# A parallel attention and GELU block: two dense groups side by side in the stretch without direct scores, an earlier fetch and another order at the end

## The chip, the cores and the metric

The kernel runs on one core of one Trainium2 chip. The metric is the device time of one execution in microseconds; of several runs the median is shown. Engines are called as in the profile: PE (matrix products), PEld (its weight loads), DVE, ACT and POOL (elementwise work), SP (which here only issues DMAs).

## What is computed

The block adds an attention and a dense part to its input. With S = 2048 rows, D = 512 columns, 32 heads of 16 columns and 1792 hidden columns:

```python
xn = layernorm(x)
q, k, v = split_heads(xn @ wqkv)                 # 32 heads, 16 columns each
p = softmax(q @ k.T * 16 ** -0.5)                # per head, 2048 x 2048
out = x + merge_heads(p @ v) @ wo + gelu(xn @ w1 + b1) @ w2 + b2
```

## The kernel before

Values that go through fp16 products are held as a high and a low half (`PAIRS`: high·high, high·low, low·high), so each product of a chunk of 128 rows is three products.

Heads go in 8 groups of four (`NG`), queries in 4 blocks of 512 (`NQB`). A pair of both is called `t`, 0 to 31; each has 16 key tiles, so there are `NU` = 512 units. A call of `unit` writes the work of one position `pos` in two halves, a = 0 and a = 1. In each half it writes, for the position's unit u, two direct scores `s_half` (tile pS, whose maxima DVE takes), for the unit 20 positions back (`LEAD`) two transposed scores `e_half` (tile pT, exponentiated by ACT into `pe`), and for a unit one or two positions further back `v_half`: the product of `pe` with the values, summed over all 16 key tiles in one bank, tile pV. Each of these uses 64 rows of the PE array and four column strips, hence four matmuls of 64x32; matmuls on rows 0 to 63 and on rows 64 to 127 are separate. In a half, pV uses the one row half.

The other row half gets `dense` work: a `Group` is one output tile in one PSUM bank, a sum over products. Its products on rows 0 to 63 and those on rows 64 to 127 are issued in alternate halves, into the same bank. `FAST`, `MEAN`, `SLOW` and `LATE` say how many half-width products a half gets, (12, 12) in the stretch after the last direct scores, so six full-width products, with four in front of pV and two behind it (`BEHIND`). One group is open at a time (`cur`). When a sum passes from one row half to the other, the first product there waits on a semaphore until the last one of the half before is done: `leave` marks the last product of a user, `enter` and `product` set the wait, for the users "V" (the pV sum) and "D" (the dense group).

PSUM has eight banks: three for tiles pS, three or four for pT, one each for a dense group and pV, passed around by `banks` and `hold`. Late dense groups take pS banks, so their tile is named pS.

Instructions stand on each engine in the order in which the code writes them. `later` and `tick` move an action some positions on, `when` does it once a head block's result is in DRAM.

The last generator of groups, `tail`, is the output projection. For a block qb of 512 rows and q in 0..3, `o_proj` multiplies the heads' result `oc` by `wo_s`. DVE adds it to `ac`, which holds the rest of the output (`finish`), and SP stores it. For blocks 2 and 3 the last 64 columns (the last heads) come too late for this, so they have a second, short group of three products, `o_end`, which reads `ol` (block 2, loaded from DRAM by `rows`) or `last` (block 3, kept in SBUF). The last head block is turned by `last_one`: four transposes, DVE's reciprocal and multiply, four transposes, ACT's and DVE's split into halves `ot`. After the last position `land` issues what is left of the open group, each row half by itself with a drain of PE ahead, and `burst` and `drain` issue whole groups on all 128 rows.

Of the kernel before, what the change touches and what calls it, by code (L numbers as in the profile page):

```python
# [18 lines left out]
S = 2048  # L19
D = 512  # L20
# [6 lines left out]
QB = 512  # L27
# [3 lines left out]
LEAD = 20  # L31
FAST, MEAN, SLOW, LATE = (8, 8), (7, 7), (6, 6), (12, 12)
MEASURE = (3, 0, 1, 2)
HALF = 1300
BEHIND = 4
POOL_NS = 2500
TAIL = 5
LFILL = (8, 16, 12, 12)
# [10 lines left out]
def layer_kernel(ctx: ExitStack, tc: tile.TileContext, x, wqkv, wo, w1, b1, w2, b2, out):  # L49
# [114 lines left out]

    turns = {u: tc.alloc_semaphore("turns" + u) for u in "VD"}
    counted, left, newest, goal = {"V": 0, "D": 0}, {}, {}, {}

# [45 lines left out]
    def later(n, fn, local=False):  # L213
        queue.append((slot[0] + n, fn, local))
# [105 lines left out]
    def v_end(u):  # L320
# [12 lines left out]
        if t == NG * NQB - 1:  # L333
            later(1, lambda: last_one(osb))
            return
# [40 lines left out]
    def last_one(osb):  # L376

        on = work.tile([P, 4, 4, DH], F32, name="on")
        rden = work.tile([P, 4, 4], F32, name="rden")
        pq = banks("S")  # L380
        for q in range(4):
            nc.tensor.transpose(pq[:, q * P:(q + 1) * P], osb[:, q * P:(q + 1) * P], ident)
        pqv = pq.rearrange("p (q h e) -> p q h e", q=4, h=4)
        nc.vector.reciprocal(rden, pqv[:, :, :, DH])
        nc.vector.tensor_tensor(on, pqv[:, :, :, 0:DH], rden.unsqueeze(3).to_broadcast([P, 4, 4, DH]), op=ALU.mult)
        pt = banks("S")
        for q in range(4):
            nc.tensor.transpose(pt[:64, q * P:(q + 1) * P], on[:, q].rearrange("p h d -> p (h d)"), ident)
        ot = work.tile([P, 2, QB], F16, name="ot", bufs=2)
        nc.scalar.activation(ot[:64, 0], pt[:64, :], AF.Copy)  # L390
        nc.vector.tensor_tensor(ot[:64, 1], pt[:64, :], ot[:64, 0], op=ALU.subtract)
        last.append(ot)

# [13 lines left out]
    def dbank():  # L407
        turn[0] += 1
        if pos[0] < LEAD:
            return banks("T"), None  # L410
        if pos[0] > NU:
            return banks("S"), None
        return hold("D", "T")

    class Group:
# [19 lines left out]
        def product(self, side, parts=2):  # L435
# [16 lines left out]
            assert not start or n == 2  # L452
            tiled("D", self.bank[:, cols], lhs[r], rhs[r][:, cols], start, self.last and self.over())
            return n
# [97 lines left out]

    pos, spent, cur = [0], [False], [None]
    feed, xbs, wcs = [], {}, {}
# [11 lines left out]

    def group(gen):

        if cur[0] is None and not spent[0]:
            cur[0] = next(gen, 0)  # L570
            if cur[0] == 0:
                cur[0], spent[0] = None, True
        return cur[0]

    def ended():

        if cur[0] is not None and cur[0].over():
            done, cur[0] = cur[0], None
            done.end()

    def burst(gen, n):

        while n > 0 and (f := group(gen)) is not None:
# [28 lines left out]
    def unit(gen):  # L612
# [7 lines left out]
        for a in range(2):  # L620
# [5 lines left out]
            if e >= 0:  # L626
# [8 lines left out]

                for user, goes_on in (("V", live and not (r == 1 and w % 16 == 15)),
                                      ("D", cur[0] is not None and not cur[0].over())):
                    leave(user, goes_on)
                for k in backlog:
# [484 lines left out]
    with ExitStack() as st3:  # L1124
# [8 lines left out]
        def fetch(qb):  # L1133
# [9 lines left out]
            for k in range(4 * qb, 4 * qb + 4):  # L1143
                if k not in acs:
                    acs[k] = p3.tile([P, D], F32, name=f"ac{k}")
                    later(2 + k % 4, lambda k=k: read_acc(acs[k], k))

        def tail():
            for qb in (2, 0, 3, 1):
                fetch(qb)  # L1150
            for qb in (2, 0, 3, 1):
                while qb != 2 and qb not in known:
                    yield None
                for q in range(4):
                    yield o_proj(qb, q, qb >= 2)

            def rows():
                nc.sync.dma_start(ol, ot_d[D - 64:, :, 2 * QB:3 * QB])
                known.add(2)

            when((NG - 1) * NQB + 2, rows)
            while 2 not in known:
# [12 lines left out]
        land()  # L1175
        while queue or steps:
            tick()
            burst(fil, TAIL)
        drain(fil)

# [26 lines left out]
```

## Time and profile before

| what | us |
|---|---|
| median of 3 runs (lowest, highest) | 1502.55 (1499.8, 1506.8) |
| profiled execution, its own time | 1504.39 |
| its span on the core | 1502.6 |
| PE busy | 1471.0 |
| DVE busy | 1374.5 |
| ACT busy | 1231.7 |
| POOL busy | 716.6 |

The span runs from the first to the last instruction of the profiled execution. The time of an execution holds a little more than the span. The mean granted clock of PE is 0.994 of full speed. Direct scores end about 1412 us into the span, the transposed scores at about 1469. A row of a timeline gives the start, the duration of the merged instructions, the engine, the line, what is written and read, and how many instructions; in brackets stands the idle time of the engine before and what ended it.

### The profile page before, as it was taken

To read this page: it belongs to the slowest core of one execution; us is meant where nothing else is said; L and a number is where in the kernel's file an instruction comes from. 1 tells how busy PE (TensorE), PEld (TensorE's weight loads), DVE (VectorE), ACT (ScalarE), POOL (GpSimd) and SP (SyncE) were. 2 spreads that over 40 slices of the span, in tenths; PEclk is the share of its full clock that TensorE was granted. 3 is DMA by queue.
4 is the path that set the end of the run, shared out by engine and by line. 5 is a ranking of instruction groups with operands and counts; after the bars stand their busy time and mean duration, and the time that the engine had idled before them with its cause. 6 is when DMAs were issued, how large, how long until landed. Compare 5 with 4: busy or idle time off the path is not lost.

```text
span 1502.6 us, 87920 instructions
## 1 busy us (share of the span) xinstructions
PE 1471.0 (98%) x39971; PEld 931.1 (62%) x39971; DVE 1374.5 (91%) x2372; ACT 1231.7 (82%) x2326; POOL 716.6 (48%) x750
## 2 busy tenths in 40 slices
PE   8998999999999999999999999999999999999997
PEld 4434566666666666666666666666666666666653
DVE  7898989999999999999999999999999999999612
ACT  5315878899999889989998998998899999988771
POOL 4113597547665545537553554665264465511000
PEclk9999999999999999999999999999999999999998
DMA  6454476633211311121112211121112111022412
GB/s 207 129 172 139 160 217 221 196 116 94 71 37 44 89 43 37 36 68 54 36 51 59 63 37 37 35 83 57 37 43 63 53 32 35 23 68 81 152 35 89
DMA packets 113677, 123.82 MB, mean 82 GB/s; under 512 B 24988, under 2 KB 85276, under 8 KB 113304
## 3 DMA queue, kind: packets, MB, share of 16 engines
q1 hardware_dynamic: 113304, 118.21, 25.5%
q8 instruction: 312, 5.11, 1.4%
q14 instruction: 61, 0.50, 0.1%
HBM read 80.61 MB, written 37.34 MB: 78 GB/s over the span
## 4 chain that ended last, share of the span: by engine, by line
PE 81%; DVE 13%; DMA 2%; issue 2%; SPq 1%; ACT 1%; POOL 0%; ACTq 0%; POOLq 0%
PE pV L170 22%; PE pD L170 20%; PE pS L170 19%; PE pT L170 17%; DVE mt L259 11%; PE pT L444 1%; PE pS L444 1%; DVE amx L679 1%; PE pT L543 1%; PE pD L444 1%; DMA m_d<-mhl 1%; PE pV L543 0%; SPq L1080 0%; DMA xs<-in_A_x_dram 0%; DVE mneg L270 0%
## 5 line engine op out<-in xcount | busy, mean ns | idle before, releaser
L259 DVE TENSOR_REDUCE mt<-pS 128x1 f32<-128x512 f32 x2048 | 1274.3, 683 | 37.4 <-PE pS L170 22.4
L304 ACT ACTIVATE pe<-pT 128x512 f32<-128x512 f32 x2048 | 1107.0, 600 | 153.3 <-PE pT L170 79.2
L170 PE MATMUL pV<-pe,vv 64*32 64x512 f32 x8192 | 1093.1, 599 | 1.1 <-issue 1.0
L170 PE MATMUL pT<-qst,kst 64*32 64x512 f16 x8192 | 668.5, 377 | 3.5 <-ACT pe L304 1.8
L170 PE MATMUL pS<-kst,qst 62*32 62x512 f16 x8192 | 632.7, 379 | 8.7 <-DVE mt L259 6.1
L170 PE MATMUL pD<-xb,wc 64*32 64x512 f16 x5376 | 372.1, 375 | 0.0
L170 PE MATMUL pD<-w_s,g 64*32 64x512 f16 (+1 forms) x6144 | 362.0, 348 | 0.0
L170 PEld LDWEIGHTS <-qst 62*32 62x32 f16 x8192 | 248.1, 92 | 140.6 <-issue 49.5
L170 PEld LDWEIGHTS <-kst 64*32 64x32 f16 x8192 | 251.8, 93 | 101.4 <-issue 13.9
L170 PEld LDWEIGHTS <-g 64*32 64x32 f16 x6144 | 196.1, 92 | 85.3 <-issue 0.7
L170 PEld LDWEIGHTS <-wc 64*32 64x32 f16 x5376 | 177.4, 91 | 98.4
L170 PEld LDWEIGHTS pV<-pe,vv 64*32 64x32 f32 x8192 | 172.5, 105 | 6.0 <-issue 2.2
L1022 POOL TENSOR_SCALAR hh<-hh,fac,b_s 128x512 f32<-128x512 f32 x56 | 43.0, 768 | 265.3 <-ACT hh L1020 265.3
L170 PE MATMUL pD<-xt,wqk_h 64*32 64x512 f16 x1920 | 129.8, 377 | 3.1 <-issue 3.0
L360 POOL TENSOR_TENSOR osb<-osb,rb 128x512 f32<-128x512 f32 x31 | 39.8, 1283 | 140.1 <-DMA rb<-den_d 101.9
L1049 POOL TENSOR_TENSOR xa<-xa,yt 128x512 f32<-128x512 f32 x32 | 41.1, 1283 | 108.4 <-ACT yt L1047 108.4
L170 PEld LDWEIGHTS <-wqk_h 64*32 64x32 f16 x1920 | 61.8, 92 | 27.7 <-issue 3.6
L1086 DVE SCALAR_TENSOR_TENSOR ac<-pS,gs,ac 128x512 f32<-128x512 f32 x20 | 15.0, 751 | 66.1 <-PE pS L170 57.2
L993 POOL TENSOR_TENSOR t<-t,hh 128x512 f32<-128x512 f32 x56 | 71.8, 1283 | 4.7
L1000 POOL TENSOR_TENSOR t<-t,hh 128x512 f32<-128x512 f32 x56 | 71.7, 1281 | 4.7
L995 POOL TENSOR_TENSOR g<-t,g 128x512 f16<-128x512 f32 x56 | 65.2, 1164 | 4.7
L170 PE MATMUL pS<-wo_s,oc 64*32 64x512 f16 x1008 | 62.6, 377 | 0.4
(140 smaller groups left out, 926.3 us busy)
## 6 DMA issues: line engine op xcount, KB each, us to landing
wch<-in_B_w_dram SPq DMA_DIRECT2D x28, 512.0 KB
wc<-w_d SPq DMA_DIRECT2D x56, 256.0 KB
qk_d<-stg SPq DMA_DIRECT2D x32, 256.0 KB
rb<-den_d SPq DMA_DIRECT2D x124, 64.0 KB
w_d<-wsp SPq DMA_DIRECT2D x28, 256.0 KB
kst<-qk_d SPq DMA_DIRECT2D x128, 48.0 KB
qst<-qk_d SPq DMA_DIRECT2D x128, 48.0 KB
xs<-in_A_x_dram SPq DMA_DIRECT2D x16, 256.0 KB
```

The lines of the kernel that those rows point to most:

```text
L170: p = nc.tensor.matmul(*args, **kw)
L259: nc.vector.reduce_max(mt_of[t][:, n, qt, kb:kb + 1], s, axis=AX.X)
L304: nc.scalar.activation(pe, st, AF.Exp, scale=factor(exp_scale, sexp[0:1, g // 2:g // 2 + 1]))
L360: pooled((1280, lambda: nc.gpsimd.tensor_tensor(osb, osb, rb, op=ALU.mult)), (620, lambda: nc.gpsimd.tensor_scalar(ot[:, 0], osb, 1.0, 0.0 ...
L444: nc.tensor.matmul(self.bank, lhs, rhs, start=start, stop=self.last and self.over())
L543: nc.tensor.matmul(pj, xt[:, i, c, t * P:(t + 1) * P], wh[j][:, c, :], start=(n == 0), stop=(n == 11))
L679: nc.vector.tensor_reduce(dst, v, axis=AX.XY if len(v.shape) == 3 else AX.X, op=ALU.max, apply_absolute_value=True)
L993: (1280, lambda: nc.gpsimd.tensor_tensor(t1, t1, hh, op=ALU.mult)),
L995: (1160, lambda: nc.gpsimd.tensor_tensor(g[:, 1, f, :], t1, g[:, 0, f, :], op=ALU.subtract)),
L1000: (1280, lambda: nc.gpsimd.tensor_tensor(t1, t1, hh, op=ALU.mult)),
L1022: later(1, lambda: pooled((690, lambda: nc.gpsimd.tensor_scalar(hh, hh, scale, bias, op0=ALU.mult, op1=ALU.add)), (0, lambda: gelu(hh, g, ...
L1049: add = lambda: nc.gpsimd.tensor_tensor(xa, xa, yt, op=ALU.add)
```

## The change

There are three edits.

1. `cur` holds two groups. After the last direct scores (`pos[0] > NU + 1`) `dense` writes three full-width products (`LATE` = 6 halves) of the first group, then pV, then three of the second, all on the same row half. A pair of groups has a user each, "D" and "E", with a semaphore and waits of its own. A lane opens a new group only where four more positions are left. `land` keeps no drain.
2. The DMA of `ol` is no longer asked for after all groups of `o_proj`, but at the start of `tail`, as soon as its rows are in DRAM.
3. `last_one` is a generator with three parts. After the last position, twelve products (`TAIL`), its first part, twelve products, its second part, then the rest of `tail` and, in a generator of its own, the four groups that read `last`.

```diff
-FAST, MEAN, SLOW, LATE = (8, 8), (7, 7), (6, 6), (12, 12)
+FAST, MEAN, SLOW, LATE = (8, 8), (7, 7), (6, 6), 6
-TAIL = 5
+TAIL = 12
...
-    turns = {u: tc.alloc_semaphore("turns" + u) for u in "VD"}
+    turns = {u: tc.alloc_semaphore("turns" + u) for u in "VDE"}
...
-            later(1, lambda: last_one(osb))
+            last.append(last_one(osb))
...
         nc.vector.tensor_tensor(on, pqv[:, :, :, 0:DH], rden.unsqueeze(3).to_broadcast([P, 4, 4, DH]), op=ALU.mult)
+        yield
         pt = banks("S")
...
-        last.append(ot)
+        last[0] = ot
+        yield
...
         if pos[0] > NU:
+            if free_banks["D"]:
+                free_banks["S"].append(free_banks["D"].pop())
             return banks("S"), None
...
-            tiled("D", self.bank[:, cols], lhs[r], rhs[r][:, cols], start, self.last and self.over())
+            tiled("DE"[cur.index(self)], self.bank[:, cols], lhs[r], rhs[r][:, cols], start, self.last and self.over())
...
+    def some_of(f, side, n, until=0):
+
+        while f is not None and n > until and f.usable(side):
+            n -= f.product(side, n)
+        return n
+
     def dense(gen, side, between=lambda: None):
 
+        if pos[0] > NU + 1:
+            fs = [group(gen, k) if cur[k] is not None or pos[0] + 4 <= NU + LEAD + 2 else None for k in range(2)]
+            some_of(fs[0], side, LATE)
+            between()
+            some_of(fs[1], side, LATE)
+            return
         f = group(gen)
-        n = 0 if f is None else (f.pace if pos[0] <= NU + 1 else LATE)[pos[0] % 2]
-        behind = 0 if f is not None and f.ends(n) else BEHIND
-        while n > behind and f.usable(side):
-            n -= f.product(side, n)
+        n = 0 if f is None else f.pace[pos[0] % 2]
+        n = some_of(f, side, n, 0 if f is not None and f.ends(n) else BEHIND)
         between()
-        while n > 0 and f.usable(side):
-            n -= f.product(side, n)
+        some_of(f, side, n)
+
+    def pass_on():
+
+        for lane, user in enumerate("DE"):
+            leave(user, cur[lane] is not None and not cur[lane].over())
 
     def land():
 
-        if cur[0] is not None:
+        for k in range(2):
             enter()
-        for side in range(2):
-            while cur[0] is not None and cur[0].left(side):
-                nc.tensor.drain()
-                while cur[0].left(side):
-                    cur[0].product(side)
+            for lane, f in enumerate(cur):
+                while f is not None and f.left((k + lane) % 2):
+                    f.product((k + lane) % 2)
+            pass_on()
         ended()
...
+        def rows():
+            nc.sync.dma_start(ol, ot_d[D - 64:, :, 2 * QB:3 * QB])
+            known.add("rows")
+
         def tail():
             for qb in (2, 0, 3, 1):
                 fetch(qb)
+            when((NG - 1) * NQB + 2, rows)
...
-            while not last:
-                yield None
+
+        def end():
             for q in range(4):
                 yield o_end(3, q, last[0])
...
         land()
+        for _ in range(2):
+            burst(fil, TAIL)
+            next(last[0])
+        drain(fil)
+        fil, spent[0] = end(), False
+        drain(fil)
         while queue or steps:
             tick()
-            burst(fil, TAIL)
-        drain(fil)
```

How the instructions move is shown at three places. On PE, in one half of a late position, the rows before are these (each weight load and matmul of a dense product stands four times; pS here is the dense group's bank, oc3 the heads' result of block 3). The first fence runs from one pV to the next half's first product.

```order
L170 MATMUL pS_48552<-wo_s_116,oc3_46698 32x512 [waits turnsD]
...
L170 MATMUL pV_48271<-pe_48506,vv_113 32x512 [waits turnsV]
...
L170 LDWEIGHTS oc3_46698
...
L170 MATMUL pT_48665<-qst1_1_3_112,kst1_1_1_94 32x512 [waits Activation_49]
...
L170 MATMUL pT_48672<-qst1_1_3_112,kst1_1_1_94 32x512 [waits Activation_49]
```

Sixteen matmuls of the group stand ahead of pV there and eight behind it. In the changed kernel a half reads so:

```order
L170 MATMUL pS_48490<-wo_s_116,oc3_46698 32x512 [waits turnsD]
...
L170 MATMUL pV_48296<-pe_48531,vv_113 32x512 [waits turnsV]
...
L170 MATMUL pS_48593<-wo_s_116,oc3_46698 32x512 [waits turnsE]
...
L170 MATMUL pT_48690<-qst1_1_3_112,kst1_1_1_94 32x512 [waits Activation_49]
...
L170 MATMUL pT_48697<-qst1_1_3_112,kst1_1_1_94 32x512 [waits Activation_49]
```

Now twelve matmuls of one bank stand ahead of pV and twelve of another behind it, with a wait of their own. On PE after the last position, before (ident marks transposes, wo_l the weights of the last 64 columns):

```order
L382 MATMUL pS_49607<-ident_74,osb_49527 128x128 x4
L388 MATMUL pS_49614<-ident_74,on_49605 64x128 x4
L444 LDWEIGHTS oc1_46703
L444 MATMUL pS_49622<-wo_s_116,oc1_46703 128x512
...
L444 MATMUL pS_49638<-wo_l_46663,ol_46665 128x512
...
L444 MATMUL pS_49662<-wo_l_46663,ot_49619 128x512
```

and now:

```order
L448 MATMUL pS_49505<-wo_s_116,oc1_46703 128x512
...
L382 MATMUL pS_49522<-ident_74,osb_49503 128x128 x4
L448 LDWEIGHTS oc1_46703
L448 MATMUL pS_49529<-wo_s_116,oc1_46703 128x512
...
L389 MATMUL pS_49544<-ident_74,on_49520 64x128 x4
L448 LDWEIGHTS ol_46665
L448 MATMUL pS_49552<-wo_l_46663,ol_46665 128x512
...
L448 MATMUL pS_49576<-wo_l_46663,ot_49549 128x512
```

Twelve products on all rows moved ahead of the first transposes and twelve between both. Ahead of the first transposes there stood 80 matmuls on single row halves. On SP before, from the write of the last heads' rows to the output stores:

```order
L367 DMA ot_d_72<-ot_48945 32x1x512 x4
L1089 DMA out_0_dram<-ac4_46704 128x512
L1089 DMA out_0_dram<-ac5_46705 128x512
L1089 DMA out_0_dram<-ac6_46706 128x512
L1089 DMA out_0_dram<-ac7_46707 128x512
L1158 DMA ol_46665<-ot_d_72 64x2x512
```

and now:

```order
L367 DMA ot_d_72<-ot_48994 32x1x512 x4
L1166 DMA ol_46665<-ot_d_72 64x2x512
L1106 DMA out_0_dram<-ac4_46704 128x512
L1106 DMA out_0_dram<-ac5_46705 128x512
L1106 DMA out_0_dram<-ac6_46706 128x512
L1106 DMA out_0_dram<-ac7_46707 128x512
```

The fetch of `ol` moved from behind four output stores to ahead of them.

More of the change, by code (lines that the diff above doesn't have):

```diff
@@ L161, in given @@
         backlog[engine] += ns
-    turns = {u: tc.alloc_semaphore("turns" + u) for u in "VD"}
-    counted, left, newest, goal = {"V": 0, "D": 0}, {}, {}, {}
+    turns = {u: tc.alloc_semaphore("turns" + u) for u in "VDE"}
+    counted, left, newest, goal = dict.fromkeys("VDE", 0), {}, {}, {}
     def product(user, *args, **kw):
@@ L551, in run @@
             pass
-    pos, spent, cur = [0], [False], [None]
+    pos, spent, cur = [0], [False], [None, None]
     feed, xbs, wcs = [], {}, {}
@@ L565, in fetch_w1, with group @@
             nc.sync.dma_start(wcs[n], w1_d[n % NF // 2, :, n % 2])
[L567 to L573, printed above, removed]
+    def group(gen, lane=0):
+        if cur[lane] is None and not spent[0]:
+            cur[lane] = next(gen, 0)
+            if cur[lane] == 0:
+                cur[lane], spent[0] = None, True
+        return cur[lane]
     def ended():
-        if cur[0] is not None and cur[0].over():
-            done, cur[0] = cur[0], None
-            done.end()
+        for lane, f in enumerate(cur):
+            if f is not None and f.over():
+                cur[lane] = None
+                f.end()
     def burst(gen, n):
@@ L634, in unit @@
                     v_half(w, r)
-                for user, goes_on in (("V", live and not (r == 1 and w % 16 == 15)),
-                                      ("D", cur[0] is not None and not cur[0].over())):
-                    leave(user, goes_on)
+                leave("V", live and not (r == 1 and w % 16 == 15))
+                pass_on()
                 for k in backlog:
@@ L1155, in tail @@
                     yield o_proj(qb, q, qb >= 2)
[L1157 to L1162, printed above, removed]
+            while "rows" not in known:
                 yield None
```

1 line of the change is left out of this document (added).

## The prediction

> **What bounds the kernel now.** I read the page first, then the windows over the end of the span, then the matmuls of one late unit in order of time, then everything after the last score.
>
> ```profile
> span 1502.6 us, 87920 instructions
> PE 1471.0 (98%) x39971; PEld 931.1 (62%) x39971; DVE 1374.5 (91%) x2372; ACT 1231.7 (82%) x2326; POOL 716.6 (48%) x750
> PE 81%; DVE 13%; DMA 2%; issue 2%; SPq 1%; ACT 1%; POOL 0%; ACTq 0%; POOLq 0%
> ```
>
> PE is the bound, but "98% busy" counts a PE on which one of the two row halves (rows 0 to 63 and 64 to 127 of the array, used by separate matmuls) works while the other stands. So I price units, not busy time. A unit issues 16 pV matmuls, so the count of pV in a window gives the length of a unit. The rows below are the windows, for tile pV alone, of the stage with direct scores and of the late stretch without them:
>
> ```profile
> 1300.00:1400.00 100.00, 81.30 (x616) 12.97 (x608) 0.00 (x0) 1.84 (x3) 1.00 0.28 85
> 1421.07:1468.98 47.91, 34.02 (x260) 5.02 (x256) 0.00 (x0) 0.60 (x1) 1.00 0.17 56
> ```
>
> 616/16 = 38.5 units in 100 us, 2.60 us each; 260/16 = 16.25 units in 47.91 us, 2.95 us each. The late unit has no direct scores and is slower. Why, the PE timeline of one late half shows (start, us, what):
>
> ```profile
> 1440.02 0.40 PE L170 MATMUL pT<-qst,kst 64*32 64x512 f16 x4
> 1440.27 0.40 PE L170 MATMUL pS<-wo_s,oc 64*32 64x512 f16 x4
> 1440.34 0.63 PE L170 MATMUL pV<-pe,vv 64*32 64x512 f32 x4
> 1440.49 0.61 PE L170 MATMUL pS<-wo_s,oc 64*32 64x512 f16 x8
> 1440.78 0.61 PE L170 MATMUL pV<-pe,vv 64*32 64x512 f32 x4
> 1440.92 0.61 PE L170 MATMUL pS<-wo_s,oc 64*32 64x512 f16 x8
> 1441.21 0.40 PE L170 MATMUL pT<-qst,kst 64*32 64x512 f16 x4
> 1441.35 0.40 PE L170 MATMUL pS<-wo_s,oc 64*32 64x512 f16 x4
> 1441.57 0.40 PE L170 MATMUL pT<-qst,kst 64*32 64x512 f16 x4
> 1441.82 0.40 PE L170 MATMUL pS<-wo_s,oc 64*32 64x512 f16 x4
> ```
>
> Dense products (pS<-wo_s,oc, four matmuls each) start 0.215 us apart (two between 1440.49 and 1440.92). The sixth starts at 1441.35 and takes about 0.38; the first of the next half starts at 1441.82, 0.09 after its end, although the transposed scores of its row half were issued at 1441.21 and held that row half for 0.215 only. That is the wait on "turnsD": the next half of the group adds to the same bank from the other row half and waits until the last product is done. A half is thus 5 x 0.215 + 0.38 + 0.09 = 1.55 us, two make 3.1; units whose second half has only three products bring the mean to 2.95.
>
> The end, all engines (rows left out are other weights and matmuls):
>
> ```profile
> 1474.74 0.61 PE L170 MATMUL pV<-pe,vv 64*32 64x512 f32 x4
> 1474.86 5.32 PE L170 MATMUL pS<-wo_s,oc 64*32 64x512 f16 x80
> ...
> 1480.11 0.66 PE L382 MATMUL pS<-ident,osb 128*128 128x128 f32 x4
> 1480.23 0.75 DVE L1086 SCALAR_TENSOR_TENSOR ac<-pS,gs,ac 128x512 f32<-128x512 f32 x1 [5.30 <-PE pS L170]
> 1480.89 0.25 DVE L384 RECIPROCAL rden<-pS 128x16 f32<-128x16 f32 x1
> 1481.75 0.60 PE L388 MATMUL pS<-ident,on 128*64 128x128 f32 x4 [0.98 <-DVE on L385]
> 1482.18 2.75 PE L444 MATMUL pS<-wo_s,oc 128*128 128x512 f16 x12
> 1482.38 0.59 ACT L390 ACTIVATE ot<-pS 64x512 f16<-64x512 f32 x1 [6.32 <-PE pS L388]
> 1483.06 0.68 DVE L391 TENSOR_TENSOR ot<-pS,ot 64x512 f16<-64x512 f32 x1 [1.46 <-DMA out_dram<-ac]
> ...
> 1486.25 0.56 SPq L1158 DMA_DIRECT2D ol<-ot_d x1
> 1489.06 4.48 PE L444 MATMUL pS<-wo_l,ol 64*128 64x512 f16 x12 [4.13 <-DMA ol<-ot_d]
> ...
> 1493.34 5.32 PE L444 MATMUL pS<-wo_l,ot 64*128 64x512 f16 x12
> ...
> 1498.70 0.75 DVE L1086 SCALAR_TENSOR_TENSOR ac<-pS,gs,ac 128x512 f32<-128x512 f32 x1 [0.53 <-PE pS L444]
> ```
>
> The last pV ends its stream at 1475.17 (the second pass at 1474.74 plus 0.43). From there to the end of the span are 27.4 us: twenty products on one row half at a time, a chain of transposes with PE waiting, then PE stands 4.13 us for the rows "ol", and the 24 products after that take 0.43 each where the twelve before (2.75 us) took 0.215. The windows over that place tell why (PE, PEld, DVE, ACT, POOL busy, then clock, DMA share, GB/s):
>
> ```profile
> 1486.00:1488.00 2.00, 0.00 (x0) 0.00 (x0) 0.00 (x0) 0.00 (x0) 0.00 (x0) 1.00 0.47 156
> 1490.00:1492.00 2.00, 2.00 (x6) 0.67 (x5) 1.42 (x2) 0.00 (x0) 0.00 (x0) 0.50 0.24 88
> 1494.00:1496.00 2.00, 2.00 (x6) 0.69 (x5) 1.08 (x2) 0.00 (x0) 0.00 (x0) 0.50 0.66 249
> ```
>
> After the idle stretch the granted clock is 0.50.
>
> **The change, part by part.** *Two groups in the late stretch.* The number of products per half stays six, three of one group before pV and three of another behind it, so nothing is removed or added but one semaphore wait per half. When a group's turn comes again, its last product lies behind three products of the other group, or behind pT, three products and pV, over 0.65 us back against the 0.47 (0.38 + 0.09) that it needs: both waits are over when they are reached. What then bounds the unit is a row half: six products, two pT and one pV (0.88 from first pass to the next matmul, 1440.34 to 1441.21), 8 x 0.215 + 0.88 = 2.60 us. The stage with direct scores puts the same on a row half (four products, two pS, two pT, one pV) and reaches exactly 2.60, with as many matmuls in a unit (80); so I take 2.60.
>
> ```profile
> 1440.31 1.08 ACT L304 ACTIVATE pe<-pT 128x512 f32<-128x512 f32 x2 [0.26 <-PE pT L170]
> ```
>
> ACT, at two exponentials in 1.08, needs 2.2 us per unit and stays hidden. 16.25 units x 0.35 = -5.7 us. Against it: two open groups and the last heads' pV leave one bank to turn over, and three groups (the third of block 0, the first two of block 3) begin in a bank whose sum DVE still has to read (0.38 + 0.75 + 0.1 = 1.2 us after the last product starts, about 1.0 away): 3 x 0.2 = +0.6. After the last transposed score at 1468.98 four pV halves are left, now 6.2 us paced by products; then each waits only for the pV before it (0.44 + 0.61 + 0.09 = 1.15): 0.3 + 3 x 1.15 + 0.88 = 4.6, -1.6. Together -6.7. Not known is how far PE passes the waits of the middle group; the ends are 0 for the units (+0.6 - 1.6 = -1.0) and, with no bank wait, -7.3. I take the upper one because the 2.60 row is the nearest.
>
> *Groups that end with the units, and twelve products between the steps of the last chain.* Nothing is left to land on single row halves, and the two drains there meet no work. After the last pV PE runs 12 full products (2.6), the four transposes (0.5), 12 products (2.6), four transposes (0.5), then 12 on "ol" and 12 on "ot". ACT's copy of the pV bank (0.6) and DVE's reciprocal and multiply lie behind the products; without that cover they would cost about 2 us. Step by step from the last pV: transposes of "on" start at 5.7; transposes to the end of DVE's "ot" took 1481.75 to 1483.74, so "ot" is done at 7.7; DVE queues the eight last sums behind it. DVE instructions back to back start 0.66 apart (1480.23, 1480.89), PE needs 0.65 per group of three, so the eighth sum ends at 7.7 + 7 x 0.66 + 0.75 = 13.1. From the end of the last sum to the end of the span were 3.15 us (1499.45 to 1502.6). Eight stores of 0.26 MB at 0.66 us ask for 397 GB/s; the row at 1494 has 249 at share 0.66, 377 at full share, so +0.4. Sum 16.7 against 27.4: -10.7. Bounds: stores that never go over 249 GB/s end 3 us later (-7.7); no crowding -11.1.
>
> *Rows fetched early.* The last of the writes that "ol" reads are these on SP's queue:
>
> ```profile
> 1454.30 3.09 SPq L367 DMA_DIRECT2D ot_d<-ot  x4
> ```
>
> The DMA "ol" moves on SP from behind four output stores to ahead of them. It waits there for the last block's rows in DRAM, whose writes are issued by 1457.4, and takes 2.8 (1486.25 to 1489.06); those rows are used at 1468.5 + 6.2 = 1474.7. The four stores behind it wait with it, and no one waits for them. It costs nothing, and its gain (4.13 idle and the slow clock) is in the 10.7. If the cover were gone, PE would stand as before.
>
> The idle stretch came before the half clock, and a stop of 0.98 us did not change it (1.00 at 1486). In the changed end no stop of PE is as long as 1 us, so I keep 0.215. The Trainium skill, "TensorE: Matmul & The Clock Gate", section "HAM oscillation — how this bites in real kernels", puts the limit at PE idle gaps of about 3.4 us; the trace agrees (4.13 us did it). The same page, in "Step-by-step: what each phase is for", states that only weight loads are pulled ahead and that matmuls stay in program order. That speaks against this change, and would make it 1493; the trace disagrees: pV stands in the queue behind four products and started at 1440.34, before the second one at 1440.49.
>
> **Sum.** -6.7 - 10.7 = -17.4 on a span of 1502.6. The profiled execution took 1504.39, 1.8 over the median 1502.55 of the runs; I subtract from the median: 1485.2.
>
> **Rivals.** (B) Products start in the order of the queue. Then pV waits for the third product (0.43), ends at 1.31, pT follows, the next half starts at 1.53, and the unit is 2 x 1.53 = 3.06: 16.25 x 0.11 = +1.8 instead of -5.7, in all 1492.7. For it: matmuls of one queue; against it the row at 1440.34. (C) The last stores or DVE pace the end: 1488, inside the range. (D) The clock falls in the end all the same: 48 products at 0.43 add 10.3, 1495.5; against it, no idle stretch of that length. (E) The other side: slower. The second group's wait stands in the middle of the half. If PE holds everything there until its queue is empty, each half pays two stops of 0.25 (0.38 - 0.215 + 0.09) and pT: 1.29 + 0.5 + 0.215 = 2.0, a unit 4.0; 19 units x 1.05 = +20, less 10.7: 1512. It decides from a unit of 2.95 + 10.7/19 = 3.5 us. Against it: today's waits on "turnsV" in the middle of each half show no such stop. That the change does nothing is excluded for the end, since "ol" and the products stand elsewhere on SP and PE.
>
> **How the numbers follow.** My forecast 0.76 (own range 1482 to 1490), B 0.10, C 0.05, D 0.04, E 0.05. The range of 1482 to 1493.5 takes in B and C and leaves out D, E and a wander of the median. Half a per cent, about what runs from 1499.8 to 1506.8 can tell, is 7.5 us, so "faster" is under 1495: 0.91 for forecast, B and C; D and part of E make the same 0.05; slower 0.04.
>
> **What would show it.** pV counts in the late stretch at 2.60 us per unit; first products of a half right behind pT; the last pV at about 1468.5; no PE stop over 1 us after it and a clock of 1.00 until DVE's last sums, which stand 0.66 apart. Wrong would be a unit near 3 us, the half clock, or sums spaced by stores.

## The result, and the profile after

The changed kernel takes 1487.59 us (median of 4 runs, 1486.93 to 1490.39) beside 1504.67 us of the kernel before (4 runs, 1499.8 to 1507.36) on the same chip: ratio 0.9884, 95% interval 0.9857 to 0.991. That is 17.1 us less; the profiled execution has a span of 1485.1 us.

The head of the page after, with the chain of waits as its last row:

```profile
span 1485.1 us, 87749 instructions
PE 1458.2 (98%) x39887; PEld 931.9 (63%) x39887; DVE 1374.0 (93%) x2372; ACT 1231.5 (83%) x2326; POOL 716.5 (48%) x750
...
PE 81%; DVE 12%; DMA 2%; issue 2%; SPq 1%; ACT 1%; POOL 0%; DVEq 0%; POOLq 0%
```

The shares hardly move. PE was "98% busy" and is so again, 17 us earlier. What changed stands in the rows of the two stages.

The PE timeline of one late unit after the change, transposed score (pT) to transposed score:

```profile
1460.16 0.52 PE L170 MATMUL pT<-qst,kst 64*32 64x512 f16 x8
1460.38 0.40 PE L170 MATMUL pS<-wo_s,oc 64*32 64x512 f16 x4
1460.47 0.64 PE L170 MATMUL pV<-pe,vv 64*32 64x512 f32 x4
1460.59 0.61 PE L170 MATMUL pS<-wo_s,oc 64*32 64x512 f16 x8
1460.90 0.64 PE L170 MATMUL pV<-pe,vv 64*32 64x512 f32 x4
1461.02 0.61 PE L170 MATMUL pS<-wo_s,oc 64*32 64x512 f16 x8
1461.33 0.43 PE L170 MATMUL pT<-qst,kst 64*32 64x512 f16 x4
...
1462.74 0.52 PE L170 MATMUL pT<-qst,kst 64*32 64x512 f16 x8
```

Halves begin at 1460.16, 1461.33 and 1462.74, so a unit is 2.58 us. The first dense product stands 0.22 behind pT, not 0.61 (1441.21 to 1441.82 before). Inside a half the products of the dense groups are 0.215 apart; across a border of the halves they are 0.09 (in the rows left out) or 0.33 apart, 0.215 in the mean, where the rows of before have 0.47. So nothing waits there for the last visit to a sum, and a row half is never without work: six products from 1460.38, then pT, pV and pT until the next product at 1462.96.

The end after, PE and DVE (rows left out are weights, other engines and single sums of DVE):

```profile
1466.77 2.21 PE L170 MATMUL pV<-pe,vv 64*32 64x512 f32 x16
1468.91 2.76 PE L448 MATMUL pS<-wo_s,oc 128*128 128x512 f16 x12
1471.52 0.60 PE L382 MATMUL pS<-ident,osb 128*128 128x128 f32 x4
1471.95 2.75 PE L448 MATMUL pS<-wo_s,oc 128*128 128x512 f16 x12
1474.54 0.60 PE L389 MATMUL pS<-ident,on 128*64 128x128 f32 x4
1475.08 2.76 PE L448 MATMUL pS<-wo_l,ol 64*128 64x512 f16 x12
...
1476.46 5.34 DVE L1103 SCALAR_TENSOR_TENSOR ac<-pS,gs,ac 128x512 f32<-128x512 f32 x8
1477.68 2.75 PE L448 MATMUL pS<-wo_l,ot 64*128 64x512 f16 x12
```

Each row of PE begins within 0.11 us of where the one above it stops streaming; no wait is shown in brackets. Every group of twelve takes 2.75 or 2.76 and the next begins 2.6 behind it, so a product takes 0.215 to the last. The eight sums take 5.34 in a row, 0.66 apart, and end at 1481.80. The windows there (PE, PEld, DVE, ACT, POOL busy, clock, DMA share, GB/s) show the full clock and output stores that keep the DMA engines busy all the time (share 0.99 and 1.01).

```profile
1478.00:1480.00 2.00, 2.00 (x11) 0.85 (x9) 2.00 (x4) 0.00 (x0) 0.00 (x0) 1.00 0.99 366
1480.00:1482.00 2.00, 0.43 (x2) 0.00 (x0) 1.81 (x3) 0.00 (x0) 0.00 (x0) 1.00 1.01 384
```

For comparing kernels I cut the last part of each span at two marks: the starts of the transposed scores at the beginning of a half. The last half of each kernel is one mark, the half forty earlier the other. Up to the first mark the kernels do the same work in the same order. "Last half to end" is the span less the second mark.

| kernel | groups late | rows | products in the chain | forty halves | last half to end |
|---|---|---|---|---|---|
| before | 1 | late | no | 1410.71 to 1468.98: 58.3 | 33.6 |
| changed | 2 | early | yes | 1409.59 to 1463.92: 54.3 | 21.2 |
| changed, once more | 2 | early | yes | 1410.70 to 1463.34: 52.6 | 21.3 |
| early rows alone | 1 | early | no | 1408.07 to 1466.34: 58.3 | 25.5 |
| rows and chain | 1 | early | yes | 1409.95 to 1468.26: 58.3 | 25.4 |
| two groups alone | 2 | late | no | 1407.47 to 1459.90: 52.4 | 34.4 |
| rows late | 2 | late | yes | 1416.34 to 1468.81: 52.5 | 28.6 |
| products late | 2 | early | no | 1411.74 to 1464.18: 52.4 | 24.3 |

### The profile page after: what moved, and what is told of

It reads as the page before. It is cut to its first block, busy times and chain, and to the rows that moved or that the text cites. A ratio compares the mean times of both kernels' runs of the same rounds, so it can differ in the third digit from the quotient of the medians.

```text
span 1485.1 us, 87749 instructions
## 1 busy us (share of the span) xinstructions
PE 1458.2 (98%) x39887; PEld 931.9 (63%) x39887; DVE 1374.0 (93%) x2372; ACT 1231.5 (83%) x2326; POOL 716.5 (48%) x750
## 4 chain that ended last, share of the span: by engine, by line
PE 81%; DVE 12%; DMA 2%; issue 2%; SPq 1%; ACT 1%; POOL 0%; DVEq 0%; POOLq 0%
PE pV L170 22%; PE pD L170 20%; PE pS L170 18%; PE pT L170 17%; DVE mt L259 10%; PE pT L448 1%; DVE amx L696 1%; PE pT L547 1%; PE pD L448 1%; PE pS L448 1%; DMA m_d<-mhl 0%; PE pV L547 0%; DMA ac<-acc_d 0%; SPq L1097 0%; DVE mneg L270 0%
## 5 line engine op out<-in xcount | busy, mean ns | idle before, releaser
L1015 POOL TENSOR_TENSOR t<-hh 128x512 f32<-128x512 f32 x56 | 58.2, 1040 | 4.1
```

The source lines that it names most:

```text
L1015: pooled((1040, lambda: nc.gpsimd.tensor_tensor(t1, hh, hh, op=ALU.mult)), (620, lambda: nc.gpsimd.tensor_scalar(t1, t1, 1.0, 1.0 / GELU_A ...
```

## The experiments

The numbers in the table are from the profiles of these runs. A ratio is to the kernel before, run in the same series on the same chip: its medians are 1506.74 us in the first series (the first four kernels here), 1506.09 in the second (the filled wait, the rows late, and the first runs of the two trimmed kernels) and 1506.54 in the third (the others). Each edit is shown against the changed kernel, or against the kernel before where the text says so; `...` stands for lines left out.

**Two groups alone.** The changed kernel with the fetch and the order at the end put back:

```diff
             for qb in (2, 0, 3, 1):
                 fetch(qb)
-            when((NG - 1) * NQB + 2, rows)
...
                 for q in range(4):
                     yield o_proj(qb, q, qb >= 2)
...
+            when((NG - 1) * NQB + 2, rows)
...
-        for _ in range(2):
-            burst(fil, TAIL)
-            next(last[0])
```

> Only the two groups side by side; the fetch of ol and the order at the end are those of before. Theory (the two parts add): the late stretch as in the changed kernel, last pV stream ending near 1468.8, unit 2.6 us; then the old end: transposes, 24 full products, a PE stop of about 4.5 us for ol, clock 0.50 and 0.43 us per product for the last 24, span 1495.3 (-7 against before). Rival (the late gain is eaten by the wait for the last heads' rows, which do not come sooner): PE stops longer and the span stays above 1500.

Measured: 1500.57 us (10 runs, 1495.25 to 1503.88), ratio 0.9961 (0.9942 to 0.9979), span 1494.3. The forty halves fall by 5.8 us and the end grows by 0.8. The end's rows on PE:

```profile
1465.73 1.11 PE L382 MATMUL pS<-ident,osb 128*128 128x128 f32 x4 [0.77 <-ACT osb L330]
1467.75 1.03 PE L388 MATMUL pS<-ident,on 128*64 128x128 f32 x4 [0.90 <-DVE on L385]
1468.57 7.28 PE L446 MATMUL pS<-wo_s,oc 128*128 128x512 f16 x24
1479.96 5.29 PE L446 MATMUL pS<-wo_l,ol 64*128 64x512 f16 x12 [4.11 <-DMA ol<-ot_d]
1485.05 5.32 PE L446 MATMUL pS<-wo_l,ot 64*128 64x512 f16 x12
```

So this part brings its gain in the stretch and loses a little in the end: the wait for "ol" (4.11) and the slow last 24 products (0.43 each) stay, and the 24 products in front of them take 0.30 each, not 0.215.

**Rows and chain, one group late.** The stretch is as before, with one group of twelve half-width products per half; early fetch and products between the steps of the chain as changed. `land` has its drains again (not shown).

```diff
-            fs = [group(gen, k) if cur[k] is not None or pos[0] + 4 <= NU + LEAD + 2 else None for k in range(2)]
-            some_of(fs[0], side, LATE)
+            f, n = group(gen), 12
+            n = some_of(f, side, 0 if f is None else n, 0 if f is not None and f.ends(n) else BEHIND)
             between()
-            some_of(fs[1], side, LATE)
+            some_of(f, side, n)
...
```

> Only the end: early fetch of ol and products between the steps of the last chain; one dense group in the late stretch, landed on single row halves with drains as before. Theory: last pV ends near 1475.2 as before, landed products to 1480, no PE stop over 1.5 us, clock 1.00, span 1494.6 (-8.0). Rival (the end is paced by the output stores): last sums end early but the span stays at 1497 or more.

Measured: 1498.01 us (6 runs, 1495.45 to 1498.82), ratio 0.9959 (0.9941 to 0.9976), span 1493.7. Its last rows on PE, behind the second transposes:

```profile
1486.52 0.60 PE L448 MATMUL pS<-wo_l,ot 64*128 64x512 f16 x2 [0.68 <-ACT ot L391]
1487.29 2.33 PE L448 MATMUL pS<-wo_l,ot 64*128 64x512 f16 x10 [0.17 <-DVE ot L392]
```

**Early rows alone.** The kernel before (the edit is against it), with only the fetch moved:

```diff
             for qb in (2, 0, 3, 1):
                 fetch(qb)
+            when((NG - 1) * NQB + 2, rows)
...
-            when((NG - 1) * NQB + 2, rows)
-            while 2 not in known:
+            while "rows" not in known:
```

> The kernel before with only the fetch of ol moved to the start of tail. Theory (the stop for ol and the clock that falls in it are nearly the whole loss of the end, and products between the steps of the chain are worth about 1 us): no stop before the products on ol, 0.215 us for each of the last 24, span 1494.4 (-8.2), the same as with the new order. Rival (the products between the steps hide the chain and are half of the gain): 1498.

Measured: 1498.12 us (10 runs, 1493.6 to 1501.33), ratio 0.9951 (0.9936 to 0.9967), span 1491.8. Its late rows on PE:

```profile
1472.21 5.32 PE L170 MATMUL pS<-wo_s,oc 64*32 64x512 f16 x80
...
1479.10 0.60 PE L388 MATMUL pS<-ident,on 128*64 128x128 f32 x4 [0.98 <-DVE on L385]
1479.54 2.75 PE L444 MATMUL pS<-wo_s,oc 128*128 128x512 f16 x12
1482.22 2.76 PE L444 MATMUL pS<-wo_l,ol 64*128 64x512 f16 x12
1484.82 2.75 PE L444 MATMUL pS<-wo_l,ot 64*128 64x512 f16 x12
```

One moved DMA takes the end from 33.6 to 25.5 us: the wait of 4.13 is gone, and with it the slow products. Adding the products between the chain's steps to this (the kernel above) brings 0.1 more (25.4). With one group late, 80 landing products run while the chain begins and cover its first step. The stop of 0.98 that is left here goes there, but then no product is left to stand behind the second transposes, and PE waits 0.68 and 0.17 for ACT's and DVE's halves of `ot` instead.

**The other order of the two groups.** The groups take turns at being first in a half, so that the group that closes one half opens the next:

```diff
-            some_of(fs[0], side, LATE)
+            some_of(fs[side], side, LATE)
             between()
-            some_of(fs[1], side, LATE)
+            some_of(fs[1 - side], side, LATE)
```

> The changed kernel, but in every other half the second group comes ahead of pV and the first behind it, so that the group that ends a half on one row half begins the next on the other. Same products, banks and semaphores. Theory (the gain of the late stretch is the wait at the border of the halves): six-product halves take 1.55 us again, about 33 of 38 halves, late stretch 54 to 57 us instead of 49.3, span 1490 to 1493. Rival (it comes from three products instead of four ahead of pV, or from two banks): late stretch 49.3, span 1485.

Measured: 1495.28 us (5 runs, 1494.28 to 1497.13), ratio 0.9934 (0.9914 to 0.9955), span 1494.6. One half of its late stretch:

```profile
1440.62 0.40 PE L170 MATMUL pT<-qst,kst 64*32 64x512 f16 x4
1440.77 0.40 PE L170 MATMUL pS<-wo_s,oc 64*32 64x512 f16 x4
1440.99 0.40 PE L170 MATMUL pT<-qst,kst 64*32 64x512 f16 x4
1441.24 0.40 PE L170 MATMUL pS<-wo_s,oc 64*32 64x512 f16 x4
...
1442.16 0.40 PE L170 MATMUL pT<-qst,kst 64*32 64x512 f16 x4
```

The half is 1.54 us again, and the sequence at the border (0.40 for the last product, the next 0.47 behind its start, at 1440.77 and 1441.24) is the one of before. Its forty halves take 60.3 us (1412.89 to 1473.20), its end 21.4 as in the changed kernel. That is 6.0 over the changed kernel's first profile and 7.7 over its second; the span lies over the 1490 to 1493 that were expected, since this stretch also begins 3.3 us later. Two open groups with the same count of products in the same banks bring nothing if a group meets itself at the border: the gain is the distance between two visits to one sum.

**Filled wait.** The kernel before (the edit is against it), with 18 products that nobody reads in the place where PE stood for "ol":

```diff
             while 2 not in known:
                 yield None
+            wp = banks("S")
+            for _ in range(18):
+                nc.tensor.matmul(wp, wo_s[:, 0, 0, 0:P], wo_s[:, 0, 0, :], start=True, stop=True)
```

> The kernel before, with 18 products of full height added whose result nobody reads; they stand behind the last twelve products of the last chain and ahead of the products that wait for the last heads' rows, and fill TensorE's wait of about 4 us there (18 x 0.215 = 3.9 us). Rows come as late as before. The theory that the idle stretch costs twice, as a wait and then as a clock that falls to half: the wait stays filled, not shortened, but the last 24 products take 0.215 us each instead of 0.43, so that the span falls by 4 to 5 us to 1497.5 to 1498.5, with a granted clock near 1.0 to the end. The rival, that the last products are slow because of what goes on beside them (stores, VectorE) and not because TensorE stood: they stay at 0.43 us and the span stays within 1 us of 1502.6.

Measured: 1502.24 us (12 runs, 1497.04 to 1506.29), ratio 0.9974 (0.9956 to 0.9992), span 1497.4.

```profile
1483.56 4.05 PE L1166 MATMUL pS<-wo_s 128*128 128x512 f16 x18
1487.85 2.76 PE L444 MATMUL pS<-wo_l,ol 64*128 64x512 f16 x12 [0.24 <-DMA ol<-ot_d]
1490.45 2.75 PE L444 MATMUL pS<-wo_l,ot 64*128 64x512 f16 x12
```

The rows come as late as before, yet the last 24 products take 0.22 each and last half to end is 29.6 instead of 33.6. So of the 8.1 us that early rows bring, 4.1 are the wait itself and 4.0 the clock that falls after it. More work on PE made the kernel 0.3% faster.

**Rows late.** The changed kernel with only the fetch put back:

```diff
             for qb in (2, 0, 3, 1):
                 fetch(qb)
-            when((NG - 1) * NQB + 2, rows)
...
                     yield o_proj(qb, q, qb >= 2)
+            when((NG - 1) * NQB + 2, rows)
             while "rows" not in known:
```

> The changed kernel with one part undone: the last heads' rows are fetched as late as before, behind the last dense group's opening; the two groups and the products between the steps of the last chain stay. The theory that the early rows carry most of the gain at the end: TensorE finds no work behind the second transposes for 3 to 4 us, the clock falls, and from the last pV to the end it takes about 24 us instead of 16.3: span 1492 to 1494. If the products between the steps keep the clock up in spite of the wait: about 19.6 us, span 1488 to 1489. The rival, that the products between the steps of the chain carry the end's gain and the rows do not matter: within 1 us of 1485.1.

Measured: 1495.58 us (7 runs, 1491.82 to 1499.22), ratio 0.9935 (0.9905 to 0.9965), span 1497.4 (its forty halves begin at 1416.34, 5 to 9 us later than those of the other kernels in the table, ahead of anything that was edited: there PE stood 2.08 us for DVE up to 1404.61, and the clock is 0.50 from 1406 to 1409).

```profile
1483.74 4.62 PE L448 MATMUL pS<-wo_l,ol 64*128 64x512 f16 x12 [3.71 <-DMA ol<-ot_d]
1488.16 5.32 PE L448 MATMUL pS<-wo_l,ot 64*128 64x512 f16 x12
```

The wait is back (3.71) and the products slow down again: 28.6 from the last half, 7.4 more than with early rows. From the last pV that is 23.7 us, where about 24 were expected; the span of 1492 to 1494 was missed by the late start. The products between the steps do not keep the clock up through such a wait.

**Products late.** The changed kernel with the last dense groups behind the chain's transposes, as before, and early rows:

```diff
-            last.append(last_one(osb))
+            later(1, lambda: last_one(osb))
...
-        for _ in range(2):
-            burst(fil, TAIL)
-            next(last[0])
```

> The changed kernel with one part undone: two groups and early rows stay, but the last dense products of block 1 stand behind the last chain's transposes, as before, not between its steps. With one group in the late stretch the interleaving was worth nothing (19.2 against 19.3 us from the last pV to the end), since 80 products of the last open group covered the chain there; with two groups that cover is gone. Theory: TensorE now stands for parts of the chain (about 0.8 and 0.9 us, and the clock gives some more: the 24 products behind it took 0.30 us each in the kernel with only the two groups), so that it takes 23 to 25.5 us from the last half to the end instead of 21.2: the interleaving is worth 2 to 4 us, ratio to the changed kernel 1.001 to 1.003. Rival one, that early rows are all there is to the end: 21 to 21.5 us. Rival two, that only the interleaving holds the clock up and it falls for the whole end: 28 us or more.

Measured: 1491.58 us (6 runs, 1488.52 to 1493.79), ratio 0.9897 (0.9876 to 0.9919), span 1488.5.

```profile
1470.02 0.65 PE L382 MATMUL pS<-ident,osb 128*128 128x128 f32 x4 [0.77 <-ACT osb L330]
1471.57 0.60 PE L388 MATMUL pS<-ident,on 128*64 128x128 f32 x4 [0.90 <-DVE on L385]
1472.00 7.03 PE L446 MATMUL pS<-wo_s,oc 128*128 128x512 f16 x24
1478.97 2.76 PE L446 MATMUL pS<-wo_l,ol 64*128 64x512 f16 x12
```

And its windows, with the clock in the third column from the right:

```profile
1471.00:1472.00 1.00, 0.43 (x4) 0.45 (x5) 0.42 (x1) 0.00 (x0) 0.00 (x0) 1.00 0.00 0
1472.00:1473.00 1.00, 1.00 (x5) 0.40 (x3) 0.12 (x1) 0.59 (x1) 0.00 (x0) 0.53 0.00 0
1473.00:1474.00 1.00, 1.00 (x4) 0.30 (x2) 0.56 (x1) 0.00 (x0) 0.00 (x0) 0.50 0.00 0
1474.00:1475.00 1.00, 1.00 (x4) 0.37 (x3) 0.00 (x0) 0.00 (x0) 0.00 (x0) 0.50 0.00 0
1475.00:1476.00 1.00, 1.00 (x5) 0.43 (x4) 0.00 (x0) 0.00 (x0) 0.00 (x0) 0.77 0.00 0
```

With two groups late the interleaving is worth 3.1 us (24.3 less 21.2): 1.7 are the stops of 0.77 and 0.90, and 1.7 are the 24 products that took 7.03 instead of 2.76 + 2.60. About 0.3 of these 3.4 does not reach the end: DVE's last sum ends 1.4 us behind PE's last product in the changed kernel, and 0.9 behind it here. The clock fell here although no stop in the chain was longer than 0.90 us. The ratio to the changed kernel, 1.0035 by the medians of this series (1491.58 and 1486.37), is a little over the 1.001 to 1.003 that were expected.

**The wait of one half at 1419.78, and the changed kernel once more.** In the first profile after the change one half took 3.04 us, for this reason (PE, then SP's queue):

```profile
1422.82 0.41 PE L170 MATMUL pT<-qst,kst 64*32 64x512 f16 x8 [1.53 <-DMA qst<-m_d]
```

```profile
1413.39 3.86 SPq L367 DMA_DIRECT2D ot_d<-ot  x4
1417.35 1.19 SPq L284 DMA_DIRECT2D m_d<-mhl  x2
1421.15 1.15 SPq L289 DMA_DIRECT2D qst<-m_d  x4
```

The transposed scores need the row maxima, which go through DRAM (m_d) into `qst`. Their store stands on SP behind four stores of head rows that took 3.86 us to issue, and the fetch follows when that store has landed. Before, the fetch was issued at 1418.77. The same kernel was run again, unaltered:

> The changed kernel once more, unaltered, on the same chip as the three others of this call, for two questions. Is the half of 3.04 us at 1419.8, which waited for the fetch of the row maxima, part of the change or of that one run? If SP's order alone sets it, it is there again; if single issues on SP that took longer made it, the forty halves before the last one take 52.4 us as in the kernel with only the two groups, instead of 54.3. The time from the last half to the end stays at 21.2 us in both.

Measured: 1486.37 us (5 runs, 1483.75 to 1489.57), ratio 0.9869 (0.9845 to 0.9893), span 1484.6. The order on SP is the same, the four stores took 3.12, the fetch was issued at 1420.20, and no half waited for it: forty halves in 52.6 us. Counted from the start of the forty halves the fetch came 2.1 us later in the first run (11.6 against 9.5): 0.7 of it are the four stores, and 1.2 the time between the end of the maxima's store on SP and the fetch (2.61 against 1.42). So the 1.7 us belong to the first run and not to SP's order, but little separates the two: the fetch was followed by its scores after 1.67 us in the first run, and in the second it was issued 1.92 us ahead of them (they start at 1422.12).

**Two trims of the changed kernel.** A PSUM bank of the transposed scores is handed to the dense groups, and the store of the maxima goes ahead on SP:

```diff
-                   (0, lambda: later(6 if t < (NG - 1) * NQB else 1, put)))
+                   (0, lambda: later(6 if t < (NG - 1) * NQB else (3 if t == NU // 16 - 3 else 1), put)))
...
+        if u == NU + 1:
+            free_banks["S"].append(free_banks["T"].pop(0))
```

It ran twice, in the second series and in the third. In the second:

> The changed kernel with two small trims: in the stretch that has only transposed scores one of the transposed scores' four PSUM banks is handed to the dense groups, so that none of them takes a bank that has just been given up; and on SP's queue the store of the row maxima and the fetch that goes back into the stacked queries stand ahead of the four stores of the head rows, not behind. Theory: the three halves of 1.55 to 1.62 us at a group's change go to 1.30 (-0.8 us), and the half of 3.04 us at 1419.8, which waited for that fetch, goes to 1.2 (-1.9 us): span 1482 to 1483, or 1484 where the runs of the changed kernel did not all have that wait. Rival: the transposed scores need their fourth bank (exp. on ScalarE gives banks back too late), the halves of the stretch grow from 1.29 to over 1.35 us and the span is at or above 1485.

Measured: 1486.52 us (6 runs, 1483.14 to 1492.12), ratio 0.9878 (0.985 to 0.9906), span 1481.4. In the third:

> The kernel of the two trims once more, beside the changed kernel on one chip. Its profile had 51.8 us for the forty halves and 21.3 us for the end, against 54.3 and 21.2 in the changed kernel's. Theory: 0.6 us of this is the bank and belongs to the kernel, the rest the run's fetch; the medians lie 0.5 to 2.5 us apart. Rival, that nothing of it can be told from the run: the intervals of the two ratios to the kernel before cover each other and the medians are within 0.5 us.

Measured: 1486.72 us (6 runs, 1482.61 to 1490.07), ratio 0.9865 (0.9843 to 0.9887), span 1483.7. The forty halves take 51.8 us in both profiles, 0.8 below the changed kernel without the wait for the fetch, as the bank's part was to be. The end stays (21.3). In the whole time it cannot be seen: 1486.72 beside 1486.37 in one series. The rival that says so holds.

**The trims, and the groups over "ol" moved forward.** They run beside the last pV products; groups of block 1 take their place in the chain, and `TAIL` is 6. The edit is shown without the two trims:

```diff
-            fs = [group(gen, k) if cur[k] is not None or pos[0] + 4 <= NU + LEAD + 2 else None for k in range(2)]
+            fs = [group(gen, k) if cur[k] is not None or pos[0] + 4 <= NU + LEAD + 2 or (pos[0] > NU + LEAD and side == 0) else None for k in range(2)]
...
                 for q in range(4):
+                    if qb == 1 and q == 2:
...
+                        for k in range(4):
+                            yield o_end(2, k, ol)
                     yield o_proj(qb, q, qb >= 2)
```

> The kernel of the two trims, and besides the four groups over the last heads' rows of block 2 are moved forward: three of them run beside the last pV products, on the row half that is idle there, and the last full groups of block 1 take their place between the steps of the last chain. Theory: 36 products of half height leave the path behind the last pV and lie beside pV products, at most 9 x 0.215 = 1.9 us of full-height time; the stores of block 2 start earlier, so that the last stores find the DMA engines less busy: 1.8 to 2.9 us less than the changed kernel beyond the trims, span 1480 to 1482. Rival: the row half that looks idle is not free (the pV products get longer, or VectorE's sums come later and hold the chain up): no more than the trims bring, 1482.5 to 1484, or worse.

Measured: 1483.52 us (6 runs, 1481.92 to 1488.47), ratio 0.9855 (0.9826 to 0.9883), span 1480.6. In the third series:

> The kernel with the trims and the groups over the last heads' rows moved forward, once more, beside the changed kernel on one chip: its profile had 18.8 us from the last half to the end instead of 21.2. Theory: 2.4 us less at the end and 0.6 in the stretch, so 3 us below the changed kernel: ratio to the kernel before 0.985 to 0.987 where the changed kernel has 0.988. Rival: no more than the run's scatter, within 1 us of it.

Measured: 1487.27 us (5 runs, 1485.93 to 1489.2), ratio 0.9873 (0.9851 to 0.9894), span 1484.1.

```profile
1466.70 0.65 PE L170 MATMUL pS<-wo_l,ol 64*32 64x512 f16 x8
...
1473.98 3.40 PE L448 MATMUL pS<-wo_s,oc 128*128 128x512 f16 x15
```

Last half to end is 18.8 us in both profiles (21.2 in the changed kernel), so 2.4 us leave the path as expected. The medians do not agree: 3.0 us under the trims in the second series, 0.9 over the changed kernel in the third (0.9873, outside the 0.985 to 0.987 that were expected), where its forty halves began at 1413.47, 2.8 us later than in the changed kernel beside it. Faster than the changed kernel by its parts; by the whole time that is not shown.

## Why the prediction was right

1485.2 us was forecast and 1487.59 measured, 17.4 and 17.1 us below the kernel before. The 2.4 between the times are nearly all the median that I subtracted from: 1502.55 in the prediction, 1504.67 in the comparison. By the marks the two parts went from 91.9 us (58.3 and 33.6) to 73.9 (52.6 and 21.3) in the changed kernel's second profile, 18.0 less, and to 75.5 in its first. In the third series, with medians of 1506.54 and 1486.37, it is 20.2 less. That 17.4 lies so near to 17.1 is in part chance.

**Units, -5.7 and +0.6.** Right. 260 pV matmuls, 16.25 units, fill the late window of the changed kernel's second profile in 42.27 us, 2.60 each with the bank waits in, where the 2.95 were:

```profile
1421.07:1463.34 42.27, 33.71 (x260) 6.95 (x256) 0.00 (x0) 0.60 (x1) 1.00 0.21 66
```

So these units take 5.6 us less, where the two terms give 5.1, and forty halves fall by as much. The steady unit is 2.58, where 2.60 was said; the trim that hands over a bank took 0.8 off, where 0.6 was said for three bank waits. In the first profile the fall is only 3.9, since one half waited for the fetch; no step of mine had that.

**Rivals B and E.** Both fall. pV at 1460.47 starts ahead of the dense product that begins a pair at 1460.59, though three products of the first group stand in front of it on the queue; a unit of 3.06 would have been two halves of 1.53, and the steady part has none of that length. What would have brought B's size is the other order of the two groups, which I had not named: 1.54 a half.

**The last pV at 1468.5.** It ends its stream at 1468.8 (1466.77 + 2.21, less the 0.18 by which 0.61 exceeds 0.43). The last four halves' share was -1.3, not -1.6: pV starts at 1464.47, 1465.62 and 1466.77, 1.15 apart as said, but the first of them 0.55 behind the last half's start, not 0.3.

**The end, 16.7.** 16.3 measured. The eighth sum was to end 13.1 us after the last pV and ended 13.0 after it; from there 3.3 us to the end of the span instead of 3.55. The stores ran at 384 GB/s with the DMA engines full, where I had scaled 249 at share 0.66 to 377. Of rival C little came: the kernel before needed 3.15 us for the last part with less crowded engines, so the crowd cost 0.2 and not 3. DVE does pace the last sums (they end 1.4 us behind PE's last product), as the forecast's own sum had it. Of D nothing is seen: the clock stays at 1.00 through the last products.

**"Without that cover they would cost about 2 us": mis-sized.** It measured 3.1. The stops are 1.7, as the rows of before led to expect. What I left out is that the clock follows them. I had argued from one stop of 0.98 us in the kernel before that stops below 1 us are harmless; there 80 products stood ahead of it. Where pV alone and two stops came one after another, the clock fell without any longer stop. The forecast did not suffer, since the changed kernel has none of these stops.

**"It costs nothing", the early rows.** Right, and larger than the sentence: alone they bring 8.1 us, and without them the changed kernel loses 7.4. The three parts do not add. Alone the early rows bring 8.1, the two groups 5.1 (58.3 to 52.4, less 0.8 at the end), the chain's products 0.1 on top of early rows. On top of early rows the two groups bring about 7 (83.8 to 76.7 by the table, both columns together): with late rows part of their gain goes into stops and slow products at the end. Two groups also take away the landing products that covered the start of the chain, and only then is the interleaving worth its 3.1.

## What to carry to other kernels

When one sum is continued across a handover, put other work between its two visits: here the order of two groups, with nothing else changed, decided between 2.58 and 3.08 us per unit. A wait of PE near the end is to be priced twice, as the wait and as the slow products behind it; moving one small DMA forward paid 8 us, half of it clock. Before calling a part of a change useless, try it with the cover gone: the same reordering was worth 0.1 us in one setting and 3.1 in the other.

## What the runs showed of the hardware

The clock also falls without a long stop. In the kernel with late products the stretch at half clock is 3.4 us long by the windows (0.94 + 1 + 1 + 0.46), after stops of 0.77 and 0.90; in the kernel with two groups alone it is 6.8 us (the clock is 0.82 in the window 1465 to 1466, 0.50 behind it, 0.76 in 1472 to 1473), and begins already during the first of the two. In the kernel with late rows a stop of 2.08 us, ahead of the late stretch, was followed by 0.50 from 1406 to 1409. The Trainium skill, "TensorE: Matmul & The Clock Gate", section "A second HAM failure mode: psum-queue depth-cycling", tells of short idles between groups of matmuls that are frequent enough to lower the clock, and "What's actually happening" of a free-running window of 3.4 us over which activity is watched; lengths of one and two such windows agree with it. What share of a window has to be idle no run here shows.

The time at which the late stretch begins wanders from 1407.5 to 1416.3 us among these profiles, ahead of every edit. That is half of the gain of the change, and more than what the last two kernels were to bring; only the marks inside one profile, which repeat within 0.3 us where no half waits for a fetch, could show them.
